# Two gate/up units split into gate and up steps, with two transposes between them

## The chip, the cores and the metric

The kernel runs on one core of one Trainium2 chip. The metric is the device time of one execution in microseconds (us). The kernel before was run three times: the median is 214.61 us, the lowest 214.41 us and the highest 215.21 us. One profiled execution took 214.28 us; the span that its profile shows, from the first to the last instruction, is 212.4 us. All times "at" which something happens are counted from the start of that span.

## The reference, cut to what matters

For 2048 tokens of width 512 the program normalises the rows, and adds three terms: the input itself, a linear attention (32 heads of 16, with exponential features), and a bilinear gated feed-forward of width 1792.

```python
x = A_x                                    # 1 x 2048 x 512, bf16
xn = _layernorm(x, axis=-1)                # (x - mean) / sqrt(var + eps), no weights
return x + _A_ref(xn, A_wqkv, A_w_phi, A_wo) + _B_ref(xn, B_w_gate, B_w_up, B_w_down)

def _B_ref(x, w_gate, w_up, w_down):       # w_gate, w_up: 512 x 1792; w_down: 1792 x 512
    g = jnp.einsum("bsd,df->bsf", x, w_gate)
    u = jnp.einsum("bsd,df->bsf", x, w_up)
    h = g * u
    return jnp.einsum("bsf,fd->bsd", h, w_down)

def _A_ref(x, wqkv, w_phi, wo):            # q, k, v = heads of x @ wqkv
    # features: softmax of +q w_phi and of -q w_phi (the same for k)  -> phi_q, phi_k
    # kv = phi_k^T v, z = sum of phi_k;  o = (phi_q kv) / (phi_q z)
    return o @ wo
```

The change lies in the first steps of the feed-forward: the products g and u of the first 256 tokens with two of the 14 column blocks of w_gate and w_up.

## The kernel before

The kernel is written as a list of named steps. Each step has an engine, a function, and the memory it reads and writes; the dependencies follow from these. A list scheduler then chooses the order of the steps on every engine, and `sc.chain("a b c")` forces a before b before c. The order is static: an engine takes its steps in that order and waits on semaphores in between. PSUM has 8 banks; a dependency is kept for a whole bank, whichever columns of it are touched.

PE is TensorE, DVE VectorE, ACT ScalarE, POOL GpSimd; SP issues most DMAs. A token tile t is 128 tokens, an FF tile ft is 128 of the 1792 columns. The normalised rows must be turned (transposed) before they can be multiplied. For token tiles 0 to 3 TensorE turns them, in two halves, each into a PSUM bank that ScalarE or VectorE then copies to SBUF (`xe`); for tiles 4 to 15 a DMA turns them (`xT`).

```python
def LN(ts, turn=True, ...):
    for t in ts:
        dve(bn_stats(...), name=f"st{t}")                       # 128x512
        dve(bn_aggr(...), name=f"ag{t}")
    act_op(lnv, var, func=Ln, bias=eps, name=f"ln{a}")          # rstd = exp(-0.5 ln(var + eps))
    act_op(rstd, lnv, func=Exp, scale=-0.5, name=f"rs{a}")
    for t in ts:
        if turn:                                                # token tiles 4 to 15
            pool(nb = -mean * rstd, name=f"nb{t}")
            act_op(xn = x * rstd + nb, name=f"nm{t}")
            sc.dma(SP, xnT, xn, turn=True, name=f"xT{t}")
            continue
        dve(xn = (x - mean) * rstd, name=f"nm{t}")              # token tiles 0 to 3

def T(t, split=False, banks=None):                              # turn by TensorE
    for hh, eng in ((0, ACT), (1, ACT if t == 0 else DVE)):
        b = nb() if banks is None else banks[hh]
        mm([... 2 matmuls of 128 columns against the identity ...], name=f"T{t}.{hh}")
        # ACT: name xe{t}a or xe{t}b;   DVE: name xe{t}d

def U2(ft, s_lo):                                               # 256 tokens, one FF tile
    b = nb()
    mm(group(bank(b, 0, 256),   [4 matmuls with w_gate])        # 8 matmuls of 256 columns, ONE bank
     + group(bank(b, 256, 256), [4 matmuls with w_up]), name=f"gu{ft}.{s_lo}")
    g = gring()[:, 0:256]
    act_op(g, bank(b, 0, 256), name=f"ge{ft}.{s_lo}")           # copy of the gate
    dve(h = bank(b, 256, 256) * g, name=f"h{ft}.{s_lo}")
# U1(ft, t): the same for one token tile (gu{ft}t{t}, ge{ft}t{t}, h{ft}t{t}; 8 matmuls of 128 columns)
# U(ft, sg): 512 tokens, gate and up in two banks (g{ft}.{sg}, u{ft}.{sg}, ge..., h...)
# ... (cut)

# the loads, in the order in which the DMA queue of SP takes them (u0 goes by ACT)
sc.chain("x0 x1 wg0 x2 wg2 wu2 wg4 wu4 wphi wT1 wv x4 wg8 wu8 x8 x12")
#   x2: token tiles 2, 3;  wg2, wu2: FF tiles 2, 3 of gate and up;  x4, x8, x12: four token tiles each

# the start
LN([0]); T(0, split=True); LN([1]); T(1, split=True)            # arguments cut
U1(0, 0); U1(1, 0); U1(0, 1); U1(1, 1)
LN([2], turn=False); LN([3], turn=False)
T(2, split=True, banks=(2, 3))
T(3, split=True, banks=(4, 5))
U2(2, 0); U2(3, 0)
rp[0] += 4
U1(0, 2); U1(1, 2); U1(0, 3); U1(1, 3); U2(2, 256); U2(3, 256)
# ... (cut: three chains, see the change)
# then: FF tiles 4 to 13 for 512 tokens (U), the folded key weights (F1), keys k0.. (K), values v0.. (V),
#       and blocks of the feed-forward by Strassen-Winograd, which need
#   XSUMS on VectorE (Xs0.0 to Xs3.1: sums of turned token tiles 4 to 11, so after xT11)
#   WSUMS on GpSimd  (gw.., uw..: sums of weight blocks)
#   b1..b7 on TensorE (b7g.0 ...), a4.., a5.. (additions) on VectorE, s.. copies on ScalarE
# K(t): k{t} on TensorE (4 matmuls of 512), ke{t} twice on ACT, kr{t} on DVE, kc{t} on ACT, kq{t}, kp{t} on POOL
# V(t): v{t} on TensorE, vs{t} on DVE, vz{t} on ACT;  KV(t): kv{t} on TensorE (needs kp{t}, vs{t})
```

Of the kernel before, what the change touches and what calls it, by code (L numbers as in the profile page):

```python
# [9 lines left out]
ALU = mybir.AluOpType  # L10
# [3 lines left out]
PE, ACT, DVE, POOL, SP = "PE", "ACT", "DVE", "POOL", "SP"  # L14
# [7 lines left out]
NQ = D // 128  # L22
# [352 lines left out]
def _build(nc, es, A_x, A_wqkv, A_w_phi, A_wo, B_w_gate, B_w_up, B_w_down, out):  # L375
# [65 lines left out]
    def bank(b, lo=0, n=512):  # L441
        return psum[:, b * 512 + lo: b * 512 + lo + n]

    sc = _Sched(nc)
# [49 lines left out]
    def mm(items, name=""):  # L494
        def fn(e):
            ins = None
            for (o, l, r, s, p) in items:
                ins = e.matmul(o, lhsT=l, rhs=r, start=s, stop=p, skip_group_check=True)  # L498
            return ins
        reads, writes, c = [], [], 0.0  # L500
        for o, l, r, s, p in items:
            track(o, s)
            reads += [l, r]
            writes.append(o)
            c += mm_cost(o.free_size())
        st = sc.step(PE, fn, reads=reads, writes=writes, cost=c, name=name)
        st.ns = tuple(o.free_size() for o, _, _, _, _ in items)
        return st

    def group(o, pairs):  # L510
        n = len(pairs)
        return [(o, l, r, i == 0, i == n - 1) for i, (l, r) in enumerate(pairs)]
# [12 lines left out]
    def xnT(q, s_lo, n):  # L525
        return xnT_v[:, q, s_lo:s_lo + n]

    wg_v = sbv("wg", 0, NQ * FF).rearrange("p (q f) -> p q f", q=NQ)
# [25 lines left out]
    def load_sq(eng, v, src, nbytes, name, after=None):  # L554
# [5 lines left out]
                      name="c")  # L560
# [76 lines left out]
    rp = [0]  # L637
# [15 lines left out]
    def T(t, split=False, banks=None):  # L653
        o = xnT_v[:, :, t * 128:(t + 1) * 128]
        if split:
            for hh, eng in ((0, ACT), (1, ACT if t == 0 else DVE)):
                b = nb() if banks is None else banks[hh]
                mm([(bank(b, q * 128, 128), xn_tile(t)[:, (2 * hh + q) * 128:(2 * hh + q + 1) * 128], ident, True, True)
                    for q in range(2)], name=f"T{t}.{hh}")
                oh = o[:, 2 * hh:2 * hh + 2, :]  # L660
                src = bank(b, 0, 256).rearrange("p (q s) -> p q s", q=2)
                if eng == ACT:
                    act_op(oh, src, name=f"xe{t}{'ab'[hh]}")
                else:
                    dve(lambda e, oh=oh, src=src: e.tensor_copy(out=oh, in_=src), [src], [oh], name=f"xe{t}d")
            return
        b = nb()
        mm([(bank(b, q * 128, 128), xn_tile(t)[:, q * 128:(q + 1) * 128], ident, True, True) for q in range(NQ)],
           name=f"T{t}")
        src = bank(b).rearrange("p (q s) -> p q s", q=NQ)  # L670
        if t % 2 == 0:
            act_op(o, src, name=f"xe{t}")
        else:
            dve(lambda e: e.tensor_copy(out=o, in_=src), [src], [o], name=f"xe{t}")
# [102 lines left out]
    def hs(s_lo):  # L777
        return s_lo % 1536
    gctr = [0]

    def gring():
        s = gctr[0] % 4
        gctr[0] += 1
        return sbv("gring", s * 512, 512)
# [132 lines left out]
    def U2(ft, s_lo):  # L917
        b = nb()
        mm(group(bank(b, 0, 256), [(wg_v[:, q, ft * 128:(ft + 1) * 128], xnT(q, s_lo, 256)) for q in range(NQ)])
           + group(bank(b, 256, 256), [(wu_v[:, q, ft * 128:(ft + 1) * 128], xnT(q, s_lo, 256)) for q in range(NQ)]),  # L920
           name=f"gu{ft}.{s_lo}")
        g = gring()[:, 0:256]
        act_op(g, bank(b, 0, 256), name=f"ge{ft}.{s_lo}")
        h = hT_v[:, ft, hs(s_lo):hs(s_lo) + 256]
        dve(lambda e: e.tensor_tensor(out=h, in0=bank(b, 256, 256), in1=g, op=ALU.mult), [bank(b, 256, 256), g], [h],  # L925
            name=f"h{ft}.{s_lo}")

    def U1(ft, t):
        b = nb()
        mm(group(bank(b, 0, 128), [(wg_v[:, q, ft * 128:(ft + 1) * 128], xnT(q, t * 128, 128)) for q in range(NQ)])  # L930
           + group(bank(b, 128, 128), [(wu_v[:, q, ft * 128:(ft + 1) * 128], xnT(q, t * 128, 128))
                                       for q in range(NQ)]), name=f"gu{ft}t{t}")
        g = gring()[:, 0:128]
        act_op(g, bank(b, 0, 128), name=f"ge{ft}t{t}")
        h = hT_v[:, ft, t * 128:(t + 1) * 128]
        dve(lambda e: e.tensor_tensor(out=h, in0=bank(b, 128, 128), in1=g, op=ALU.mult), [bank(b, 128, 128), g], [h],
            name=f"h{ft}t{t}")
# [166 lines left out]
    U1(1, 1)  # L1104
    LN([2], turn=False)
    LN([3], turn=False)
    T(2, split=True, banks=(2, 3))
    T(3, split=True, banks=(4, 5))
    U2(2, 0)
    U2(3, 0)  # L1110
    rp[0] += 4
    U1(0, 2)
    U1(1, 2)
    U1(0, 3)
    U1(1, 3)
    U2(2, 256)
    U2(3, 256)
    sc.chain("st0 ag0 st1 ag1 nm0.0 nm0.1 nm1 xe1d st2 ag2 h0t0 st3 ag3 nm2 h1t0 nm3 xe2d xe3d h0t1")
    sc.chain("T3.1 gu3.0")
    sc.chain("ln0 rs0 ln1 rs1 xe0a xe0b xe1a ge0t0 ln2 rs2 ge1t0 ln3 rs3 xe2a xe3a")  # L1120
    late = [len(sc.steps)]
    units = [(U, ft, 0) for ft in range(4, NF)]
    n0 = len(units)
# [166 lines left out]
```

The softmax here doesn't subtract the row's maximum and nothing guards it: scores larger than these inputs give would overflow.

## Time and profile before

| | |
|---|---|
| median of 3 runs | 214.61 us (214.41 to 215.21) |
| span of the profile | 212.4 us |
| granted TensorE clock | full speed in every slice |
| idle share: PE, DVE, ACT, POOL | 3%, 25%, 46%, 28% of the span |
| HBM read, written | 9.72 MB, 2.10 MB |
| costliest group | the matmuls: 201.2 us busy in 1597 records |
| next | GpSimd sums of 128x256 and larger (L766): 108.2 us busy in 96 records |

How to read it: an engine's busy share is an average over stages that have different limits, and a busy TensorE is not one at its peak, since matmuls are pipelined and their ends are modelled. A line of a timeline gives the start, the busy length, the engine, the line of the kernel and the shape; in brackets stand the idle time of the engine just before it and what ended that idle time. L498 is the line of every matmul, L451 of every ScalarE operation, L631 that of the normalising of token tiles 0 to 3 (`nm`), L796 that of `h` of U, L853 that of `a4` and `a5`, L925 that of `h` of U2, L716 that of `kp`. "SPq" is SP's queue that issues DMAs.

### The profile page before, as it was taken

How to read it: one execution, taken by the hardware profiler on the slowest of the kernel's cores; microseconds unless marked ns; L12 is line 12 of the kernel's file. 1: busy time of each engine (PE TensorE's matmuls, PEld its weight loads, DVE VectorE, ACT ScalarE, POOL GpSimd, SP SyncE). 2: the span in 40 equal slices, each digit the busy share in tenths (PEclk: the TensorE clock that was granted, in tenths of full speed). 3: DMA queues.
4: the chain of work that ended last, by engine and by line, in shares of the span. 5: the costliest groups of instructions: out<-in, count | busy, mean ns of one | idle time of the engine just before them, and what ended most of it. 6: DMA issues, size and time to landing. Idle time of an engine off the chain costs nothing.

```text
span 212.4 us, 4261 instructions
## 1 busy us (share of the span) xinstructions
PE 205.5 (97%) x1607; PEld 137.4 (65%) x1630; DVE 159.3 (75%) x313; ACT 113.8 (54%) x292; POOL 153.2 (72%) x191
## 2 busy tenths in 40 slices
PE   8799999999999999999999999999999999999995
PEld 3585444543454444444456788898888888888984
DVE  4655599899977698889987875686666876568653
ACT  4646998789796959697822533424433244332000
POOL 4060589359999999999999795875958779422640
PEclk9999999999999999999999999999999999999999
DMA  5999634793200000222620246143261434624421
GB/s 164 328 241 376 205 79 76 233 287 99 44 8 0 3 0 0 49 51 52 209 39 3 49 52 149 25 101 75 55 146 25 94 84 76 119 51 84 99 76 52
DMA packets 49718, 21.01 MB, mean 99 GB/s; under 512 B 37409, under 2 KB 49697, under 8 KB 49697
## 3 DMA queue, kind: packets, MB, share of 16 engines
q1 hardware_dynamic: 49024, 20.41, 39.9%
q10 hardware_dynamic: 672, 0.33, 0.6%
q8 instruction: 13, 0.21, 0.4%
q14 instruction: 9, 0.07, 0.1%
HBM read 9.72 MB, written 2.10 MB: 56 GB/s over the span
## 4 chain that ended last, share of the span: by engine, by line
PE 68%; POOL 23%; DMA 3%; issue 2%; SPq 1%; DVE 1%; ACT 0%; DVEq 0%; POOLq 0%
PE ps L498 68%; POOL arena L766 16%; POOL arena L716 6%; DMA arena<-in_B_w_up_dram 3%; POOL arena L714 1%; SPq L175 1%; DVE arena L925 0%; ACT arena L451 0%; POOL arena L621 0%; DVE arena L1015 0%; DVE arena L631 0%; DVEq L349 0%; DVE arena L1078 0%; POOLq L320 0%
## 5 line engine op out<-in xcount | busy, mean ns | idle before, releaser
L498 PE MATMUL ps<-arena 128*128 128x256 bf16 (+5 forms) x1597 | 201.2, 286 | 3.7 <-DVE arena L631 1.2
L498 PEld LDWEIGHTS ps<-arena 128*128 128x128 bf16 (+1 forms) x1620 | 136.0, 98 | 69.4 <-DVE arena L631 2.1
L766 POOL TENSOR_TENSOR arena<-arena 128x256 f16<-128x256 bf16 (+3 forms) x96 | 108.2, 1148 | 22.9 <-PE ps L498 16.9
L451 ACT ACTIVATE arena<-ps 128x512 bf16<-128x512 f32 (+3 forms) x167 | 83.7, 535 | 68.5 <-PE ps L498 66.5
L707 DVE TENSOR_REDUCE arena<-arena 128x64 f32<-128x1024 bf16 x32 | 38.7, 1211 | 9.4 <-ACT arena L451 9.4
L451 ACT ACTIVATE arena<-arena 128x32 f32<-128x32 f32 (+4 forms) x96 | 28.9, 317 | 12.8 <-DVE arena L707 10.2
L716 POOL TENSOR_TENSOR arena<-arena 128x512 bf16<-128x512 bf16 x32 | 34.2, 1072 | 0.7
L1015 DVE TENSOR_TENSOR arena<-ps,arena 128x256 f32<-128x256 f32 (+1 forms) x56 | 23.4, 420 | 12.6 <-PE ps L498 12.3
L925 DVE TENSOR_TENSOR arena<-ps,arena 128x256 f16<-128x256 f32 x32 | 13.4, 419 | 11.2 <-ACT arena L451 11.2
L847 DVE TENSOR_TENSOR arena<-ps,arena 128x512 f16<-128x512 f32 x24 | 16.1, 683 | 1.0 <-PE ps L498 0.8
L714 POOL TENSOR_TENSOR arena<-arena 128x32 f32<-128x32 f32 x32 | 8.7, 275 | 9.3 <-ACT arena L451 9.3
L612 DVE BATCH_NORM_STATS2 arena<-arena 128x6 f32<-128x512 bf16 x16 | 10.6, 674 | 3.4 <-DMA arena<-in_A_x_dram 3.4
L741 DVE TENSOR_TENSOR arena<-ps,arena 128x512 bf16<-128x512 f32 x16 | 10.8, 680 | 2.1 <-ACT arena L451 1.5
L796 DVE TENSOR_TENSOR arena<-ps,arena 128x512 f16<-128x512 f32 x14 | 9.5, 680 | 2.9 <-PE ps L498 1.8
L853 DVE TENSOR_TENSOR ps<-ps,arena 128x512 f32<-128x512 f32 x12 | 8.1, 694 | 4.4 <-PE ps L498 2.9
L973 DVE TENSOR_TENSOR arena<-ps,arena 128x512 bf16<-128x512 f32 x16 | 11.0, 688 | 0.4
L621 POOL TENSOR_SCALAR arena<-arena 128x1 f32<-128x1 f32 x12 | 3.5, 314 | 8.5 <-ACT arena L451 8.5
L853 DVE TENSOR_TENSOR arena<-ps,arena 128x512 bf16<-128x512 f32 x12 | 8.0, 678 | 0.0
L594 POOL TENSOR_TENSOR arena<-arena 128x128 bf16<-128x128 bf16 x4 | 1.6, 427 | 8.8 <-DMA arena<-in_A_w_phi_dram 8.8
L451 ACT ACTIVATE ps<-ps 128x512 f32<-128x512 f32 x12 | 7.2, 598 | 0.6 <-PE ps L498 0.6
L969 DVE RECIPROCAL arena<-arena 128x32 f32<-128x32 f32 x16 | 5.6, 351 | 0.4
L1092 PE MATMUL ps<-const-bfloat16-1.0 128*128 128x512 bf16 x10 | 4.4, 629 | 0.8 <-PEq L1275 0.8
(21 smaller groups left out, 27.9 us busy)
## 6 DMA issues: line engine op xcount, KB each, us to landing
arena<-in_A_x_dram SPq DMA_DIRECT2D x5, 512.0 KB, 6.9
arena<-in_B_w_down_dram SPq DMA_DIRECT2D x1, 1792.0 KB, 8.1
out_dram<-arena SPq DMA_DIRECT2D x14, 128.0 KB, 2.1
arena<-in_B_w_gate_dram SPq DMA_DIRECT2D x1, 768.0 KB, 8.5
arena<-in_B_w_up_dram SPq DMA_DIRECT2D x1, 768.0 KB, 10.0
arena<-arena SPq DMA_TRANSPOSE x44, 3.0
arena<-in_B_w_gate_dram SPq DMA_DIRECT2D x2, 256.0 KB, 4.7
arena<-in_B_w_gate_dram SPq DMA_DIRECT2D x1, 512.0 KB, 6.3
```

The lines of the kernel that those rows point to most:

```text
L451: return e.activation(out=out_ap, in_=in_ap, func=func, scale=scale, **kw)
L498: ins = e.matmul(o, lhsT=l, rhs=r, start=s, stop=p, skip_group_check=True)
L707: dve(lambda e, ei=ei, so=so: e.tensor_reduce(out=so, in_=ei.rearrange("p (h f) -> p h f", f=16), axis=AX.X, op=ALU.add), [ei], [so], cost ...
L714: pool(lambda e: e.tensor_tensor(out=ratio, in0=smv[:, :, 0], in1=rc, op=ALU.mult), [sm, rc], [ratio], 225.0, name=f"{name}q{t}")
L716: pool(lambda e: e.tensor_tensor(out=ev[:, :, 1, :], in0=ev[:, :, 1, :], in1=ratio[:, :, None].to_broadcast([128, H, 16]), op=ALU.mult), [ ...
L741: dve(lambda e: e.tensor_tensor(out=o1, in0=src, in1=rp_[:, :, :, None].to_broadcast([128, 8, 4, 16]), op=ALU.mult), [src, rs_v[:, t % 4, ...
L766: fn = lambda e: e.tensor_tensor(out=out_, in0=a_, in1=b_, op=op)
L847: dve(lambda e: e.tensor_tensor(out=h, in0=src, in1=g, op=ALU.mult), [src, g], [h], name=f"h{ft}.{sg}", prio=PD)
L853: dve(lambda e: e.tensor_tensor(out=o, in0=src, in1=sn, op=ALU.add), [src, sn], [o], name=name, prio=PD)
L925: dve(lambda e: e.tensor_tensor(out=h, in0=bank(b, 256, 256), in1=g, op=ALU.mult), [bank(b, 256, 256), g], [h], name=f"h{ft}.{s_lo}")
L973: dve(lambda e: e.tensor_tensor(out=ov, in0=src, in1=wv4[:, :, :, None].to_broadcast([128, 8, 4, 16]), op=ALU.mult), [src, w], [o], cost=6 ...
L1015: dve(lambda e: e.tensor_tensor(out=out_, in0=in_ps, in1=in_sb, op=ALU.add), [in_ps, in_sb], [out_], cost=328.0, name=f"{name}.{p}")
```

## The change

The first 256-token units of FF tiles 2 and 3 (`U2(2, 0)` and `U2(3, 0)`, 8 matmuls in one bank each) become four steps of 4 matmuls, gate and up in banks of their own. The two gate steps no longer need the up weights (`wu2`), which arrive one DMA later than the gate weights; the turns of token tiles 2 and 3 are put between the up steps. The chains for the three engines are rewritten: on TensorE the order is fixed outright; on ScalarE `rs3` (the scale of token tile 3) goes ahead of `ge2.0`; on VectorE `nm3` goes ahead of `h2.0`. The second half of token tile 2 is copied out by ScalarE (`xe2b`) and no longer by VectorE (`xe2d`). The numbers of the banks that follow shift by three places in the ring. It is meant to give TensorE work in its two early waits.

```diff
     def T(t, split=False, banks=None):
-            for hh, eng in ((0, ACT), (1, ACT if t == 0 else DVE)):
+            for hh, eng in ((0, ACT), (1, ACT if t in (0, 2) else DVE)):
...
+    def GU2(fts, s_lo, bg, bu, order):
+        g = {ft: gring()[:, 0:256] for ft in fts}
+        for w, ft in order:
+            if w == "T":
+                T(ft, split=True, banks=bu["T"][ft])
+                continue
+            b = bank((bg if w == "g" else bu)[ft], 0, 256)
+            v = wg_v if w == "g" else wu_v
+            mm(group(b, [(v[:, q, ft * 128:(ft + 1) * 128], xnT(q, s_lo, 256)) for q in range(NQ)]),
+               name=f"{w}{ft}.{s_lo}h")
+            if w == "g":
+                act_op(g[ft], b, name=f"ge{ft}.{s_lo}")
+            else:
+                h = hT_v[:, ft, hs(s_lo):hs(s_lo) + 256]
+                dve(lambda e, h=h, b=b, gg=g[ft]: e.tensor_tensor(out=h, in0=b, in1=gg, op=ALU.mult), [b, g[ft]], [h],
+                    name=f"h{ft}.{s_lo}")
...
     LN([2], turn=False)
     LN([3], turn=False)
-    T(2, split=True, banks=(2, 3))
-    T(3, split=True, banks=(4, 5))
-    U2(2, 0)
-    U2(3, 0)
-    rp[0] += 4
+    GU2((2, 3), 0, {2: 0, 3: 1}, {2: 4, 3: 5, "T": {2: (2, 7), 3: (3, 6)}},
+        [("g", 2), ("g", 3), ("u", 2), ("T", 2), ("u", 3), ("T", 3)])
+    rp[0] += 7
...
-    sc.chain("st0 ag0 st1 ag1 nm0.0 nm0.1 nm1 xe1d st2 ag2 h0t0 st3 ag3 nm2 h1t0 nm3 xe2d xe3d h0t1")
-    sc.chain("T3.1 gu3.0")
-    sc.chain("ln0 rs0 ln1 rs1 xe0a xe0b xe1a ge0t0 ln2 rs2 ge1t0 ln3 rs3 xe2a xe3a")
+    sc.chain("g2.0h g3.0h u2.0h T2.0 T2.1 u3.0h T3.0 T3.1 gu1t2")
+    sc.chain("st0 ag0 st1 ag1 nm0.0 nm0.1 nm1 xe1d st2 ag2 h0t0 st3 h1t1 ag3 nm2 h1t0 nm3 h0t1 h2.0 xe3d h3.0")
+    sc.chain("ln0 rs0 ln1 rs1 xe0a xe0b xe1a ge0t0 ln2 rs2 ge1t0 ln3 rs3 ge2.0 xe2a xe2b xe3a ge3.0")
```

The orders that the scheduler makes of it at the start are these (names of steps; no times are in them):

```
TensorE before:  gu0t0 gu1t0 gu0t1 gu1t1 | gu2.0 | T2.0 T2.1 | T3.0 T3.1 | gu3.0 | gu1t2 gu0t2 gu0t3 gu1t3 gu2.256 gu3.256
TensorE after:   gu0t0 gu1t0 gu0t1 gu1t1 | g2.0h g3.0h | u2.0h | T2.0 T2.1 | u3.0h | T3.0 T3.1 | gu0t2 gu1t2 gu0t3 gu1t3 gu2.256 gu3.256
ScalarE before:  ... ge1t0 ln3 ge2.0 rs3 xe2a xe3a ge3.0 ...
ScalarE after:   ... ge1t0 ln3 rs3 ge2.0 xe2a xe2b xe3a ge3.0 ...
VectorE before:  ... nm2 h1t0 h2.0 nm3 xe2d xe3d h0t1 h3.0 ...
VectorE after:   ... nm2 h1t0 nm3 h0t1 h2.0 xe3d h3.0 ...
```

The same scheduler places everything that follows, so later orders move too. On TensorE the sequence from kv4 to v14 is the same in both, k1 moves ahead of u8.0, and a few steps near kv14, kv15 and n0 to n2 change places. On ScalarE and GpSimd the keys' steps, the weight sums and the normalising of tiles 4 to 15 are interleaved differently: on ScalarE the two `ke0` now stand together ahead of `nm4`, `nm12` stands behind `kc3l` (the first half of `kc3`) and `nm13` behind `s7g.0`; on GpSimd `nb8` stands behind `gw2.0` as before, but with `gw3.1` moved ahead of it, and `S1.0` (a sum for the last product) stands ahead of `kq4` and no longer behind it.

## The prediction

> **What bounds the kernel now.** I read the page first, then the timeline of the first 16 us, then the waits and the timeline of each engine up to 96 us. The first part of the page says which engine is full:
>
> ```profile
> PE 205.5 (97%) x1607; PEld 137.4 (65%) x1630; DVE 159.3 (75%) x313; ACT 113.8 (54%) x292; POOL 153.2 (72%) x191
> ```
>
> TensorE is idle for 6.9 us in all. So the change can win only where TensorE is idle, and what it wins counts only if TensorE doesn't idle later instead. The chain of work that ended last agrees: 68% of it is TensorE, 23% GpSimd, which stands in it from 42 to 95 us. The timeline of the start shows the two waits that the change aims at:
>
> ```profile
> 8.64 1.27 PE L498 MATMUL ps<-arena 128*128 128x256 bf16 x12 [0.52 <-DMA arena<-in_B_w_up_dram]
> ...
> 8.81 0.38 DVE L631 TENSOR_SCALAR arena<-arena 128x512 bf16<-128x512 bf16 x1
> 8.93 0.29 ACT L451 ACTIVATE arena<-arena 128x1 f32<-128x1 f32 x1 [0.23 <-DVE arena L614]
> 9.11 0.28 DVE L936 TENSOR_TENSOR arena<-ps,arena 128x128 f16<-128x128 f32 x1
> 9.73 0.38 ACT L451 ACTIVATE arena<-ps 128x256 bf16<-128x256 f32 x1 [0.51 <-PE ps L498]
> 10.01 0.19 ACT L451 ACTIVATE arena<-arena 128x1 f32<-128x1 f32 x1
> ...
> 10.14 0.42 DVE L925 TENSOR_TENSOR arena<-ps,arena 128x256 f16<-128x256 f32 x1 [0.76 <-ACT arena L451]
> 10.48 0.40 DVE L631 TENSOR_SCALAR arena<-arena 128x512 bf16<-128x512 bf16 x1
> ...
> 10.94 21.24 PE L498 MATMUL ps<-arena 128*128 128x128 bf16 x146 [1.03 <-DVE arena L631]
> ```
>
> In brackets stands the idle time and what ended it. TensorE waits 0.52 us for the up weights (gu2.0), and 1.03 us for nm3, the row at 10.48. That row is late because ScalarE did ge2.0 (9.73) before rs3 (10.01), and VectorE did h2.0 (10.14) before nm3. After 10.94 TensorE hardly idles; the later waits, from the timelines of SP, VectorE and TensorE, are these:
>
> ```profile
> 31.21 6.25 SPq L174 DMA_TRANSPOSE arena<-arena  x4
> ...
> 38.77 1.43 DVE L766 TENSOR_TENSOR arena<-arena 128x512 f16<-128x512 bf16 x4 [0.55 <-DMA arena<-arena]
> ...
> 42.88 5.55 PE L498 MATMUL ps<-arena 128*128 128x512 bf16 x31 [0.27 <-DVE arena L796]
> 48.67 1.68 PE L498 MATMUL ps<-arena 128*128 128x512 f16 x7 [0.23 <-DVE arena L853]
> ...
> 95.36 1.51 PE L498 MATMUL ps<-arena 128*128 128x68 bf16 x12 [0.17 <-POOL arena L716]
> ```
>
> The reader should see a second chain: turns xT8 to xT11 by DMA, then the sums Xs0.0 to Xs1.1 on VectorE at 38.77, then h13.0, for which k5 on TensorE waits, then a4g.0, for which b7u.0 waits. By stretches:
>
> ```profile
> 26.00:38.00 12.00, 11.95 (x56) 5.46 (x56) 12.00 (x24) 11.01 (x30) 11.21 (x21) 1.00 0.41 78
> 38.00:39.00 1.00, 1.00 (x7) 0.47 (x5) 0.46 (x2) 1.00 (x3) 0.00 (x0) 1.00 0.28 33
> 39.00:52.00 13.00, 12.50 (x78) 5.82 (x78) 13.00 (x23) 11.05 (x31) 8.07 (x12) 1.00 0.89 242
> 52.00:62.00 10.00, 9.89 (x69) 4.94 (x70) 7.98 (x13) 8.78 (x21) 10.00 (x18) 1.00 0.14 28
> ```
>
> The columns after the length are PE, PEld, DVE, ACT, POOL. VectorE has no idle time from 26 to 38 us and from 39 to 52 us, 12.00 of 12 and 13.00 of 13. There it is as much a bound as TensorE is, and the only gap between is the wait for xT11. That decides my prediction.
>
> **What the Trainium skill says.** "PSUM — Partial Sum Buffer", section "Engine vs sequencer instructions": the queues of ScalarE, VectorE and GpSimd are strictly first in, first out, and matmuls start and complete in program order. The trace agrees: nm3 sat behind h2.0 and TensorE idled 1.03 us. "Perfetto Trace Analysis", section "Matmuls": independent groups should rotate through PSUM banks, so that one is read out while the next is computed. Here ge2.0 starts at 9.73, after all eight matmuls of gu2.0 (the last ends at 9.69), although its four were done sooner; banks of their own end that. "TensorE: Matmul & The Clock Gate", section "Wait — 56ns, not 53.3ns?": a warm matmul takes N / 2.4 GHz plus 2.5 ns, so 56 ns for 128 columns and 109 ns for 256, an estimate from that page. The trace agrees: eight of 256 and four of 128 come to 1.10 us, and the row at 8.64 shows 1.27 us with the tail of the last one (0.22 us).
>
> **The change, part by part.** Matmuls, copies and multiplications stay as many as before; one 128x256 copy moves from VectorE (0.42 us) to ScalarE (0.38 us), and that work isn't on the path. So only waits move. I walk the new orders with the durations above.
>
> Start. The last matmul of gu1t1 is issued at 7.91, and wg2 landed at 7.8 (issued at 2.75, 5.0 us). So g2.0h and g3.0h run from 7.97 to 8.84, 8 x 0.109. wu2 landed at 8.60: u2.0h to 9.28. T2 needs nm2, which ends at 9.19: T2 to 9.50. u3.0h to 9.94 (its bank is freed by h1t0 at 9.39). rs3 now follows ln3 at once and ends at 9.46; nm3 runs after h1t0 from 9.52 to 9.91; T3.0 starts at 9.96; T3.1 waits for h0t1 (to 10.11) and is issued by 10.27. On ScalarE ge2.0, xe2a and xe2b then follow at 9.38, 9.67 and 9.96 + 0.38 = 10.34, so gu0t2 starts at 10.39. In the kernel before the same work (gu1t2) starts at 12.05, which is 10.94 + 4 x 0.056 + 8 x 0.109. Gain so far 1.65 us: the two waits are 0.52 + 1.03 us by the brackets, and 0.16 us more each from issue to issue, since the brackets leave out the tail of the matmul before (1.87 us); about 0.2 us are lost to new waits for nm3, h0t1 and xe2b.
>
> From 14 to 37 us. The weights wg4 to wu8 land before they are needed (wu8 at 23.4, u8.0 at 24.3), k0 still finds fe13 just ready, and I find no new wait over 0.25 us. TensorE stays 1.4 to 1.65 us ahead.
>
> The chain of token tiles 8 to 11 doesn't come with it. x4 lands at 19.19 and x8 at 24.81 (issued at 14.38, 10.4 us), whatever TensorE does. On ScalarE ln4 starts at 21.3, not at 21.87, since it waits for x4 by st4, st5 and ag5. On VectorE st8 moves from 26.56 to 26.0. On GpSimd nb8 stands behind gw3.0, gw1.0, gw3.1 and gw2.0 (0.64 us each), which wait for nm7 (26.8): nb8 ends at 30.0. So nm8 starts at 30.1 and not at 30.36, and the four turns of SP, which take 6.25 us in a row and are bound by themselves after the first, start 0.25 us sooner. xT11 lands at 38.5 and not at 38.75.
>
> From 38.5 to 49 us. VectorE has the same work in the same order up to kr4: h13.0 ends 3.83 us after the start of Xs0.0 (42.60 - 38.77), so at 42.3. TensorE reaches k5 at 41.0 and waits 1.3 us. There the gain falls from about 1.4 to 0.25 us. Then st15 (0.6 us) comes ahead of a4g.0 and vs4 behind it, which cancel, and nm13 delays sdg.0 on ScalarE; b7u.0 starts at 48.5 and not at 48.67. I keep 0.15 us.
>
> At 95.36. TensorE waits for kp12; its previous matmul was issued 0.36 us before and takes 0.03, so kv12 could start at 95.03. GpSimd is full from 49 us on, so its order decides. Adding the durations of the trace before in each order from the first of kq4 and S1.0 to the end of kp12 gives 48.1 us before and 47.2 us after. S1.0 may start at 47.15 (after xT13, which is late because nm13 is), 0.27 us later than kq4 did. So kp12 ends some 0.6 us sooner, and the wait of 0.3 us goes. Slacks of kv13 to kv15 and n0 to n3 are 0.3 to 2.5 us before, and I find none that turns into a wait.
>
> Sum: 0.15 + 0.3 = 0.45 us, from 214.61 to 214.15 us.
>
> **The rivals.** First: the gain of the start goes through whole. For it speaks that TensorE is full after 11 us and the DMA weights are early. Against it stands VectorE's 13.00 of 13 us, which begins with a landing that doesn't move. It would be so if the turns took less: xT8's issue took 2.3 of the 6.25 us, the other three 1.3 each, and without that the landing comes 1.1 us sooner. It would make 213.0 to 213.4 us. Second: the start is won and lost twice, because ScalarE now waits for kr3 (behind kc3l) ahead of nm12 and ke4, so that b1g.0 and b2g.0 wait in their turn, and S1.0 holds kq4 back until xT13. It would leave nothing or cost up to 0.5 us: 214.6 to 215.1 us. Third: T3.1's and xe2b's waits are longer than walked, so that the start gains 1 us and not 1.65. It changes nothing at the end, because 1.3 us are waited away at k5.
>
> **Range and chances.** I expect 214.15 us. The first rival reaches to 213.2, the second to 214.9, and I give the middle most of the weight. 2% are 4.3 us, nearly three times what TensorE could gain even if both waits went whole; and no step adds work. So within 2% is all but sure: 0.98.
>
> **What would show it.** In the profile after: no idle time of TensorE from 8 to 9.5 us, and at most 0.3 us to 10.5; the first 128-column matmuls after T3 at about 10.4. Idle time of VectorE before Xs0.0 over 1 us, ended by a DMA, with Xs0.0 at 38.5. TensorE idle over 1 us before k5, at about 42.4, ended by L796. No wait for L716 near 95. I am wrong if Xs0.0 starts before 37.8 (first rival), or if TensorE has idle time over 0.3 us at more places than k5 between 42 and 62 us (second rival).

## The result, and the profile after

| kernel | median | lowest to highest | executions |
|---|---|---|---|
| before | 214.65 us | 214.16 to 215.21 | 6 |
| after | 213.28 us | 212.32 to 213.53 | 6 |

The medians lie 1.37 us apart, where 0.45 us had been predicted. The ratio is 0.9929, with a 95% interval of 0.9903 to 0.9954; ratios in this document are not quotients of the medians (0.9936 here), so the two differ a little. The profile of the kernel after is of the slowest of its six executions (213.53 us), that of the kernel before of one of 214.28 us. In the chain of work that ended last, which the page gives by engine, GpSimd had 23% of the span and has 4% now; TensorE has 78% instead of 68%. This is that line of the kernel after:

```profile
PE 78%; ACT 7%; DMA 5%; POOL 4%; DVE 3%; issue 1%; SPq 0%; DVEq 0%
```

The start, from the timeline of TensorE (first row) and that of all engines in the kernel after (start, duration, engine, line, operands; idle time before it in brackets):

```profile
6.80 6.46 PE L498 MATMUL ps<-arena 128*128 128x128 bf16 x90
...
9.35 0.53 ACT L451 ACTIVATE arena<-arena 128x1 f32<-128x1 f32 x2 [0.19 <-DVE arena L614]
...
9.78 1.30 ACT L451 ACTIVATE arena<-ps 128x256 bf16<-128x256 f32 x4
9.91 0.41 DVE L631 TENSOR_SCALAR arena<-arena 128x512 bf16<-128x512 bf16 x1
```

The reader should see that TensorE's row runs from 6.80 to 13.26 us without a bracket. Both waits of the kernel before (0.52 us at 8.64, 1.03 us at 10.94) are gone. ln3 and rs3 stand together at 9.35, ahead of ge2.0 at 9.78, and nm3 starts at 9.91 instead of 10.48.

The later rows that answer to those shown of the kernel before, from the timelines of SP, VectorE and TensorE:

```profile
30.54 5.13 SPq L174 DMA_TRANSPOSE arena<-arena  x4
...
36.98 1.84 DVE L766 TENSOR_TENSOR arena<-arena 128x512 f16<-128x512 bf16 x4 [0.22 <-DMA arena<-arena]
...
47.24 9.93 PE L498 MATMUL ps<-arena 128*128 128x512 f16 x52 [0.31 <-DVE arena L853]
57.49 2.82 PE L498 MATMUL ps<-arena 128*128 128x512 bf16 x25 [0.33 <-ACT ps L451]
89.75 10.61 PE L498 MATMUL ps<-arena 128*128 128x512 bf16 x62
```

The four turns xT8 to xT11 are issued in 5.13 us and not in 6.25 us, and start 0.67 us sooner. So the sums on VectorE (36.98) start 1.79 us sooner than in the kernel before (38.77). There is no wait worth a row at k5 (0.10 us from issue to issue), a longer one at b7u.0 (47.24), a new one at b2u.1 (57.49, for ScalarE), and none near 94 us, where the kernel before waited for kp12. Putting the starts of single steps of TensorE side by side gives the account:

| step | before | after | difference | what lies between |
|---|---|---|---|---|
| gu0t0 | 6.18 | 6.64 | +0.46 | wg0 landed at 6.55 and not 6.09 |
| first of gu0t2, gu1t2 | 12.05 | 10.76 | -1.29 | both early waits gone |
| kv1, the step ahead of k5 | 42.20 | 40.92 | -1.28 | nothing lost in 30 us |
| k5 | 42.66 | 41.27 | -1.39 | its wait for h13.0 shrank from 0.2 to 0.1 us |
| b7u.0 | 48.67 | 47.24 | -1.43 | wait for a4g.0 in both |
| b2u.1 | 58.43 | 57.49 | -0.94 | new wait, 0.49 us from issue to issue |
| kv12 | 95.36 | 94.11 | -1.25 | wait for kp12 (0.33 us from issue to issue) gone |
| last group (W22.7) | 209.58 | 208.32 | -1.26 | |

In the kernel before the record of k5's first matmul is missing; its weight load stands at 42.65, and the row at 42.88 is the second matmul.

By stretches (columns after the length: PE, PEld, DVE, ACT, POOL busy) the kernel after is:

```profile
26.00:38.00 12.00, 12.00 (x57) 5.44 (x56) 11.78 (x24) 11.32 (x29) 10.65 (x19) 1.00 0.45 89
...
39.00:52.00 13.00, 12.69 (x73) 5.63 (x72) 12.52 (x20) 11.61 (x32) 7.54 (x12) 1.00 0.73 203
```

VectorE is still all but full there, as the prediction had it. What was wrong is when its work arrives.

### The profile page after: what moved, and what is told of

Its sections match the earlier page's. It is cut to its first block, busy times and chain, and to the rows that moved or that the text cites. A ratio compares the mean times of both kernels' runs of the same rounds, so it can differ in the third digit from the quotient of the medians.

```text
span 211.2 us, 4288 instructions
## 1 busy us (share of the span) xinstructions
PE 206.6 (98%) x1630; PEld 137.1 (65%) x1630; DVE 159.9 (76%) x312; ACT 114.3 (54%) x293; POOL 153.1 (73%) x191
## 4 chain that ended last, share of the span: by engine, by line
PE 78%; ACT 7%; DMA 5%; POOL 4%; DVE 3%; issue 1%; SPq 0%; DVEq 0%
PE ps L498 78%; ACT arena L451 6%; DMA arena<-arena 3%; DMA arena<-in_B_w_gate_dram 2%; POOL arena L766 2%; POOL arena L716 1%; DVE arena L612 1%; DVE arena L766 1%; DVE arena L707 1%; SPq L175 0%; DVE arena L796 0%; POOL arena L714 0%; ACT ps L451 0%; DVE arena L614 0%; DVE arena L1032 0%
## 5 line engine op out<-in xcount | busy, mean ns | idle before, releaser
L498 PE MATMUL ps<-arena 128*128 128x512 bf16 (+5 forms) x1620 | 202.4, 287 | 1.3 <-DMA arena<-in_B_w_gate_dram 0.4
L498 PEld LDWEIGHTS ps<-arena 128*128 128x128 bf16 (+1 forms) x1620 | 135.7, 98 | 68.4 <-ACT arena L451 2.2
L451 ACT ACTIVATE arena<-ps 128x512 bf16<-128x512 f32 (+3 forms) x168 | 83.3, 533 | 66.0 <-PE ps L498 62.8
L451 ACT ACTIVATE arena<-arena 128x64 f32<-128x64 f32 (+4 forms) x96 | 28.5, 314 | 14.2 <-DVE arena L707 10.9
L925 DVE TENSOR_TENSOR arena<-ps,arena 128x256 f16<-128x256 f32 x30 | 12.6, 418 | 9.5 <-ACT arena L451 9.5
L451 ACT ACTIVATE ps<-ps 128x512 f32<-128x512 f32 x12 | 7.2, 600 | 0.0
```

The source lines that it names most:

```text
L451: return e.activation(out=out_ap, in_=in_ap, func=func, scale=scale, **kw)
```

## Why xT8 is quicker: the theories

xT8 is of the same size in both kernels. From its issue to its landing it takes 4.31 us before (31.21 to 35.52) and 2.41 us after (30.54 to 32.95). The DMA view of the kernel before, for the 4 us from the issue of xT8 in 40 slices of 0.1 us (busy share in tenths, then GB/s, then the kinds of packets):

```profile
DMA  0000810000006999999601000000001000003999
GB/s 0 0 0 0 164 82 0 0 0 0 0 8 138 212 228 215 205 156 123 15 8 5 5 18 10 10 15 5 0 5 8 3 0 0 0 0 82 215 210 236
...
q8 instruction: 1, 0.02, 2.2%
q14 instruction: 2, 0.02, 2.2%
```

And the same for the kernel after, from 30.5 us on:

```profile
DMA  0000030000004999995200000399999520000029
GB/s 0 0 0 0 0 82 0 0 0 0 0 0 90 210 228 225 212 207 115 24 0 0 0 0 0 72 200 225 223 212 215 133 32 0 0 0 0 0 51 197
...
q14 instruction: 1, 0.01, 0.8%
```

After, each turn is one burst of 0.7 us, and the next follows 1.3 us later. Before, the burst of xT8 ends in a trickle of 3 to 18 GB/s, from 33.1 to 34.4 us, the next burst only comes at 34.8, and xT8 is complete inside it, at 35.52. In the same window lies a packet of q8 (16 KB in slice 5, the 164 GB/s). The page counts 13 packets of q8. "Runtime: NRT & Kernel Launch", section "Instruction fetch mechanics", of the Trainium skill says that a sequencer fetches its instructions by a DMA queue of its own, in blocks of 16 KiB or 256 instructions. TensorE has 1,630 matmuls and as many weight loads, 3,260 or 12.7 blocks, so q8 should be TensorE's. The traces agree: the second packet of q8 comes when 208 to 214 weight loads have started, the warm-up's included, which with as many matmuls are 416 to 428 instructions, in all fourteen profiled executions, and in the kernel before the packets after it follow 254 instructions apart in the mean. q14 carries packets of 8 KB; that they are the other engines' is taken from their size and not shown. TensorE's block was fetched at 31.66 us before, 0.45 us after the issue of xT8, and at 30.21 us after, 0.33 us ahead of it.

Theory A: a fetch that falls into a turn holds it up. The fetch goes with TensorE's place in its program, so the change moves it out of xT8. Theory B: landings vary by chance. Theory C: the new order of everything after 14 us brings xT8 forward. Later, rival D: the whole gain is the moved fetch and the change has no part in it.

## The experiments on the fetch

**The kernel before once more, unchanged.** It shows how far executions of one program differ.

> The kernel before, unchanged, profiled a second time. Theory A (the turn xT8 took 2.3 us in the first profile because an instruction fetch of TensorE fell into it, which the order of the program fixes): xT8 takes about 2.3 us again, the four turns xT8 to xT11 6.2 us in a row, Xs0.0 on VectorE starts at 38.5 to 39. Theory B (the landing of the loads x4 and x8 varies from execution to execution, and the first profile caught a late one): xT8 takes 1.2 to 1.3 us or x4 lands a microsecond elsewhere, and Xs0.0 starts at 37 to 38. Time: ratio 1.000 in both.

Measured: 214.23 us (213.25 to 215.19, 22 executions), ratio 1.0002 [0.9990, 1.0014]. The profiled execution was its quickest (213.25 us). In it the fetch fell at 32.09, xT8 took 4.39 us to land, but xT9 to xT11 lost less, and xT11 landed at 38.12 and not 38.75. VectorE, which has work up to that moment, didn't wait at all, nor did TensorE at k5 or b7u.0, and W22.7 started at 208.55, 1.03 us sooner. So executions of one program lie up to 1.9 us apart, and in the quickest the turns landed sooner, with the fetch inside xT8 all the same: what counts for the time is when xT11 lands. Half of the 22 lie between 214.0 and 214.5 us: chance is real, and does not explain a median that moves.

**The fetch moved in the kernel before.** Six more, shorter warm-up matmuls bring TensorE's block limit forward; everything else is the same.

```diff
-    WARM(10)     # matmuls of 512 columns
+    WARM(16)     # matmuls of 320 columns
```

> The kernel before with its warm-up of 10 matmuls of 512 columns cut into 16 of 320: the same columns in the same time, but 6 matmuls and 6 weight loads more ahead of everything, so that TensorE's instruction fetch that came at 31.7 us comes about 1.3 us sooner, at 30.4, ahead of xT8 at 31.2. All orders are those of the kernel before. Theory A: xT8 takes 1.2 us, Xs0.0 starts about 1.1 us sooner (37.6), the waits at k5 and b7u.0 shrink, and the time falls by 0.5 to 0.9 us (ratio 0.9958 to 0.9977). Theory B and theory C (the new order after 14 us is what brings xT8 forward): ratio 1.000.

Measured: 213.30 us (212.93 to 213.48, 6 executions), ratio 0.9954 [0.9942, 0.9965]. The fetch came at 30.88; xT8 landed after 3.52 us, xT11 at 37.91. VectorE had no gap before Xs0.0 (38.07), and the waits at k5 and b7u.0 were gone. The timeline of SP:

```profile
31.13 5.49 SPq L174 DMA_TRANSPOSE arena<-arena  x4
```

The start is as it was (g4.0 at 15.51, 15.58 before). The ratio is a little better than theory A said, without a line of the change: B falls, and C isn't needed for this part. But the steps came short of what A said: the fetch lay 0.25 us ahead of xT8 and not 0.8, the issue of xT8 took 1.53 us and not 1.2, and Xs0.0 started at 38.07 and not 37.6.

**The fetch moved back in the kernel after.** The warm-up is three matmuls shorter and starts later.

```diff
-    WARM(10)
+    WARM(7)      # and the first waits for a constant
```

> The changed kernel with a warm-up of 7 matmuls and no longer 10, the first held back until GpSimd has made a mask (at about 2.2 us), so that it ends when it ended before; 3 matmuls and 3 weight loads fewer, so that TensorE's fetch at 30.2 comes about 0.65 us later, at 30.9, inside xT8 (30.5 to 31.7). All orders are those of the changed kernel. Theory A: xT8 takes 2.3 us, xT11 lands 1.1 us later, TensorE waits about 1 us at k5, and the time is 0.6 to 1.1 us over that of the changed kernel (ratio to the kernel before 0.9965 to 0.999). Theory B and C: the time of the changed kernel (ratio 0.993).

Measured: 212.89 us (212.51 to 213.64, 6 executions), ratio 0.9939 [0.9924, 0.9955]. The median misses what A expected and is what B and C expected. But the profiled execution was the slowest of the six (213.64 us), and in it the fetch fell into xT8, at 32.17. Its timelines:

```profile
30.95 6.20 SPq L174 DMA_TRANSPOSE arena<-arena  x4
...
38.45 1.43 DVE L766 TENSOR_TENSOR arena<-arena 128x512 f16<-128x512 bf16 x4 [1.29 <-DMA arena<-arena]
...
42.57 5.42 PE L498 MATMUL ps<-arena 128*128 128x512 bf16 x31 [0.82 <-DVE arena L796]
48.29 11.92 PE L498 MATMUL ps<-arena 128*128 128x512 f16 x73 [0.30 <-DVE arena L853]
```

This is the picture that was predicted: the turns in 6.2 us, VectorE idle for over 1 us before Xs0.0, which starts at 38.45 (predicted 38.5), TensorE waiting 0.82 us at k5 (over 1 us predicted), b7u.0 at 48.29 (predicted 48.5). So the prediction described an execution that this order can have when the fetch falls into xT8. The other five were 0.36 to 1.13 us quicker; where their fetch fell was not profiled.

**The fetch moved further, in both kernels.** Twenty warm-up matmuls of 256 columns, in one set of runs on one chip, so that the change can be compared with itself.

```diff
-    WARM(10)     # matmuls of 512 columns
+    WARM(20)     # matmuls of 256 columns, in before and in after
```

> The kernel before with its warm-up as 20 matmuls of 256 columns (ten instructions more), so that TensorE's instruction block is fetched near 30.4 us, clear ahead of the issue of xT8 at 31.15. Theory A (only a fetch that falls into the turn holds it): xT8 lands 2.4 us after its issue as in the kernel after (4.3 us in the kernel before), xT11 by 37.5 us; but VectorE has work up to 38.07 us anyway, so the time is that of the edit with 16 matmuls, 0.994 to 0.9965 of the kernel before, with W22.7 at 208.4 to 208.6. Rival B (landings vary by chance, the fetch has no part): xT8 lands 3.5 to 4.4 us after its issue and the time is 0.998 to 1.001.

> The kernel after with the same warm-up of 20 matmuls; the fetch falls near 28.9 us, into xT7, which nothing waits for yet. With the kernel before under the same edit, on the same chip, this gives what the change gains when neither has the fetch in xT8. Theory A: 0.3 to 0.7 us less than the kernel before with 20 matmuls, 0.991 to 0.994 of the kernel before. Rival D (all of the gain was the fetch): no difference within 0.15 us. Rival E (the change gains as much with the fetch out of the way, and the fetch's gain comes on top): over 1.0 us less.

Measured: the kernel before 214.47 us; before with 20 matmuls 213.33 us (213.24 to 213.47, 6 executions), 0.9939 [0.9915, 0.9962]; after with 20 matmuls 212.52 us (211.84 to 212.86, 5 executions), 0.9891 [0.9859, 0.9922]. Between the two edited kernels lie 0.81 us, and no execution of one reaches the other's range. So D falls. The value lies between what A and E expected, over A's 0.7 and under E's 1.0 us by the medians; between the two profiled executions (W22.7 at 208.59 and 207.40) it is 1.19 us. In round numbers, of 1.95 us 1.14 come with the shifted fetch and 0.81 with the change. In the kernel after without this edit the two can't be cut so cleanly, since the change itself moves the fetch. One expectation missed: with 20 matmuls in the kernel before, xT8 took 3.38 us and not 2.4. The fetch now fell into xT7 (4.17 us), which landed 1.37 us after xT8 was issued, and two packets of q14 fell into xT8; which of the two held it was not separated. The timeline of TensorE in the kernel after with 20 matmuls:

```profile
6.80 6.40 PE L498 MATMUL ps<-arena 128*128 128x128 bf16 x86
...
46.83 13.45 PE L498 MATMUL ps<-arena 128*128 128x512 f16 x82 [0.31 <-DVE arena L853]
```

Here wg0 landed at 6.08, gu0t0 started at 6.23, and the gain at the start is 1.68 us (g4.0 at 13.91, 15.59 without the change). The wait at b2u.1 didn't occur. The wait at b7u.0 remains: with smaller ones before it, it takes the lead over the kernel before with 20 matmuls from 1.68 us at kv1 to 0.85 us at b7u.0; at b2u.1 the lead is 1.06 us.

**The kernel after with 16 matmuls.**

> The kernel after, with only the warm-up of TensorE written as 16 matmuls of 320 columns instead of 10 of 512 (same columns, six instructions more), so that TensorE's instruction block is fetched some 0.9 us earlier. The kernel before with the same edit was at 0.9954 [0.9942, 0.9965] of the kernel before. Theory A (the change gains by itself, and the fetch only takes from it what it hits): 0.989 to 0.993 of the kernel before, 0.6 to 1.2 us under the kernel before with the same edit, and no different from the kernel after, whose fetch already lies before xT8. Rival D (the whole gain of the change was that its six extra or earlier instructions moved the fetch): 0.995 to 0.996, no faster than the kernel before with the same edit.

Measured: 212.94 us (212.71 to 213.49, 7 executions), 0.9936 [0.9913, 0.9959]. That lies between what A (up to 0.993) and D (from 0.995) expected, and the 0.9954 of the kernel before with the same edit comes from another chip; so this run by itself leaves D open, and the pair above was run. In the profiled execution wg0 landed late (7.02 us, gu0t0 at 7.11). The fetch fell into xT7, which took 4.28 us and which nothing waited for; xT8 took 2.40.

All profiled executions together, by what was fetched between 0.3 us ahead of xT8's issue and its landing:

| fetched beside xT8 | executions | issue to landing of xT8, us | issue of xT8 to landing of xT11, us |
|---|---|---|---|
| one q14, no q8 | 4 (after; after with 16 and 20; after tuned) | 2.41, 2.40, 2.64, 2.40 | 6.41, 6.40, 6.67, 6.40 |
| q8 within 0.3 us ahead, or two q14 | 3 (before with 16 and 20; last version below) | 3.52, 3.38, 3.20 | 6.77, 6.77, 6.78 |
| q8 up to 1.3 us after the issue | 7 (before, twice; after with 7; the other four below) | 4.30, 4.39, 4.11, 3.31, 4.10, 4.08, 4.04 | 7.53, 6.94, 7.48, 7.30, 7.32, 7.53, 7.26 |

The last column is what Xs0.0 waits for. It is not the order of the engines that parts the rows: with the order of the kernel after it is 6.40 to 6.67 us in the four without the fetch and 7.48 us in the one with it (7 matmuls). The limit of 0.3 us was drawn with the results in view: the kernel after has its fetch 0.33 us ahead of xT8 and the turn isn't held, the last version has it 0.27 us ahead and it is. Four of the seven had two packets of q14 besides; the three with one took 4.11, 3.31 and 4.04 us.

And xT7 took 2.46 to 2.48 us in eleven of the fourteen; in the three where TensorE's block was fetched beside it, it took 4.28, 4.17 and 3.86.

## The experiments on the parts of the change

In these kernels and in those of the next part, the orders of all engines are fixed by a list, so that only the named steps move; line numbers shift for it (TensorE's L498 is L585 to L587, ScalarE's L451 is L538 to L540).

**The new start with the old order from 14 us on.** On TensorE, ScalarE and VectorE the order of the kernel before from g4.0, ge4.0 and h4.0 on, on GpSimd and SP throughout.

```diff
- ... the scheduler's order after the change
+ sc.pin(PIN)   # start as after; from g4.0 / ge4.0 / h4.0 on as before
```

> The changed kernel with its new start, but from g4.0, ge4.0 and h4.0 on (and on GpSimd and SP throughout) in the order of the kernel before. Theory A: TensorE's fetch comes at about 30.2 with TensorE 1.3 to 1.7 us ahead, xT8 at 30.6 to 31.2, so they don't meet; xT11 lands by 37.6 and the ratio is 0.993 to 0.996. Theory C (the new order of ScalarE and GpSimd after 14 us brings xT8 and xT11 forward): TensorE waits about 1 us at k5 and the ratio is 0.997 to 1.000. Theory B: anything between.

Measured: 212.71 us (212.39 to 213.06, 5 executions), 0.9926 [0.9913, 0.9938]. That is the ratio of the kernel after. Theory C falls: the new order downstream isn't needed. Theory A is close in the ratio and missed a step: the fetch at 30.16 did meet xT8, which was issued at 29.77 and took 3.31 us. The timelines of SP and VectorE:

```profile
29.77 6.02 SPq L174 DMA_TRANSPOSE arena<-arena  x4
...
37.10 1.43 DVE L854 TENSOR_TENSOR arena<-arena 128x512 f16<-128x512 bf16 x4 [0.37 <-DMA arena<-arena]
```

The four turns took 6.02 us, and Xs0.0 still came at 37.10, because nm8 started at 28.93 us (before 30.36, after 29.72), though GpSimd's order was that of the kernel before.

**Only the two orders, no split.**

```diff
-    ... ln3 ge2.0 rs3 xe2a ...      (ScalarE)      ... h2.0 nm3 ...   (VectorE)
+    ... ln3 rs3 ge2.0 xe2a ...      (ScalarE)      ... nm3 h2.0 ...   (VectorE)
```

> The kernel before, all orders pinned as they were, but rs3 ahead of ge2.0 on ScalarE and nm3 ahead of h2.0 on VectorE. Nothing is split, no bank changes. Theory A (waits are what counts, and one of the two can be taken without the split): nm3 ends near 9.9 us, T3.0 starts at about 9.96 instead of 10.94, the wait of 0.52 us for the up weights stays, g4.0 starts at about 14.5 instead of 15.58, gain about 1.0 us at the start; at the end 0.4 to 1.0 us less than the kernel before, ratio 0.9953 to 0.998. Rival (the reorder only hands the wait on, because h2.0 then holds gu3.0's bank or T2's copies): T3.0 near 10 us but g4.0 not under 15.2 us, ratio over 0.998.

Measured: 213.09 us (212.35 to 213.37, 6 executions), 0.9930 [0.9905, 0.9956]. T3.0 started at 9.80 and g4.0 at 14.52, as theory A said; at the end it gained more than A said. The timeline of TensorE:

```profile
8.58 3.63 PE L585 MATMUL ps<-arena 128*128 128x256 bf16 x43 [0.57 <-DMA arena<-in_B_w_up_dram]
...
47.60 14.57 PE L585 MATMUL ps<-arena 128*128 128x512 f16 x99 [0.24 <-DVE arena L940]
```

The wait for wu2 stays, the one for nm3 is gone, and the ratio can't be told from that of the kernel after. Here too the fetch fell into xT8 (4.10 us). Two swaps of neighbours do, as the kernel stands, what the split does.

**Only the split.** ge2.0 ahead of rs3 and h2.0 ahead of nm3 as in the kernel before, and its order from g4.0 on; split, banks and TensorE's order as after.

```diff
-    ... ln3 rs3 ge2.0 ...           (ScalarE)      ... nm3 h0t1 h2.0 ...   (VectorE)
+    ... ln3 ge2.0 rs3 ...           (ScalarE)      ... h2.0 nm3 h0t1 ...   (VectorE)
```

> The kernel after with its split, banks and TensorE order, but ge2.0 ahead of rs3 on ScalarE and h2.0 ahead of nm3 on VectorE as in the kernel before, and the order of before from g4.0 on. Theory A (splitting the units fills both waits even without the other order, because ge2.0 is ready 0.9 us sooner when the gate step has a bank of its own): T3.0 at about 10.3 us, g4.0 at 14.25 to 14.5 us, gain at the start 1.1 to 1.3 us; ratio 0.992 to 0.995. Rival (the order of nm3 is what counts, the split alone only moves the wait to T3): T3.0 at 10.7 us or later, g4.0 at 14.9 or later, ratio over 0.996.

Measured: 213.30 us (213.06 to 213.59, 8 executions), 0.9949 [0.9931, 0.9968]. wu2 landed late (9.23 us, 8.60 before), so that u2.0h waited. T3.0 came at 10.88, as late as the rival said, g4.0 at 14.73, between the two, and the time is A's.

The three show one more thing. With the order of the kernel before downstream, g4.0 came 1.49, 1.06 and 0.85 us sooner than in the kernel before, and nm8 came 1.43, 1.08 and 0.86 us sooner: one for one. In the order of the kernel after it is 1.28 and 0.65 us (with 20 matmuls 1.68 and 1.04 against the edited kernel before). The chain of token tiles 8 to 11 does come along; the new order (gw3.1, 0.67 us, stands ahead of nb8 there) only holds back some 0.6 us of it. And it follows TensorE, not the load: with the fetch shifted and nothing else, in the kernel before, x4 landed at 17.84 us (16 matmuls) and 18.19 us (20 matmuls) and no longer at 19.19, and ln4, the first step of token tiles 4 and 5 on ScalarE, came at 21.79 and 21.87 us (21.87 before), and xT8 was issued at 31.13 and 31.22 us.

## The experiments on what is given back

**The kernel after with three pairs of steps moved.**

```diff
-    ag14 st15 kr5 a4g.0 vs4 a5g.0 ag15 h0.1 kr6           (VectorE)
+    ag14 kr5 a4g.0 vs4 a5g.0 h0.1 kr6 st15 ag15
-    s2g.1 nm14 nm15 ke7 ke7 sdu.1 ge1.2 s7u.1 kc7l s2u.1 sdg.2          (ScalarE)
+    s2g.1 ke7 ke7 sdu.1 ge1.2 s7u.1 kc7l s2u.1 nm14 nm15 sdg.2
```

> The kernel after, its orders pinned, with st15 and ag15 moved behind kr6 on VectorE (so that a4g.0 is done 0.6 us sooner) and nm14 and nm15 moved behind s2u.1 on ScalarE. Theory A (the waits of 0.48 us at b7u.0 and 0.49 us at b2u.1 are what the change gives back): both waits go, W22.7 starts 0.5 to 0.9 us sooner than in the kernel after, ratio 0.989 to 0.991. Rival (VectorE and GpSimd are full there and hand the wait on: a5g.0, or tiles 14 and 15 come late): waits of the same size at b5u.0, at the steps of tiles 14 and 15, or at kv12, and a ratio of 0.992 to 0.995, as the kernel after.

Measured: 213.72 us (213.43 to 214.22, 22 executions), 0.9972 [0.9963, 0.9982]: slower than the kernel after. The rival came true in kind, at other places than it named and at a higher price (it had said 0.992 to 0.995). The timeline of TensorE:

```profile
51.43 8.04 PE L587 MATMUL ps<-arena 128*128 128x512 bf16 x56 [0.35 <-ACT ps L540]
60.48 1.70 PE L587 MATMUL ps<-arena 128*128 128x512 bf16 x12 [1.01 <-ACT ps L540]
```

The wait at b7u.0 fell from 0.48 to 0.07 us and that at b2u.1 went. In their place TensorE waits for sdg.1 (ln14 ahead of it now waits for ag15) and for sdg.2 (nm14 and nm15 now stand ahead of it). Both edits won their wait and paid for it on the same engine a few steps on, 1.9 us in all with a small wait at F0 behind them.

**The old order downstream, tuned, with and without the shifted fetch.**

```diff
-    ke5 kc4l kc4 ge0.1 s2g.0 sdu.0   (ScalarE)   kr5 vs4 a4g.0   (VectorE)   kq4 S1.0   (GpSimd)
+    ke5 ge0.1 s2g.0 sdu.0 kc4l kc4   (ScalarE)   kr5 a4g.0 vs4   (VectorE)   S1.0 kq4   (GpSimd)
```

> The start of the kernel after with the order of before from g4.0 on, and three moves: on ScalarE ge0.1, s2g.0 and sdu.0 ahead of kc4l and kc4, which wait for kr4 of VectorE; on VectorE a4g.0 ahead of vs4; on GpSimd S1.0 ahead of kq4. Theory A (ScalarE stood 1.10 us before kc4l while s2g.0 was ready, and that made the waits of 0.34 us at b5g.0 and 0.40 us at b7u.0): the wait at b5g.0 goes, that at b7u.0 falls under 0.15 us, S1.0 starts at 44.8 us instead of 45.6, so GpSimd's kp12 comes about 0.6 us sooner too, W22.7 at 207.3 to 207.7, ratio 0.989 to 0.992. Rival (the wait is handed on as in the other tuned version): waits of over 0.3 us between 48 and 62 us or over 0.6 us at kv12, no faster than 0.9926.

> The same with the warm-up as 16 matmuls of 320 columns. Theory A (the fetch at 30.16 us still held xT8, which landed 3.3 us after its issue): the fetch comes near 29.3 us, xT8 lands near 32.2 us, VectorE doesn't wait before Xs0.0 (0.37 us), and the time is another 0.1 to 0.4 us down: ratio 0.987 to 0.991. Rival (GpSimd's chain up to kp12 sets the end by now): the same time as without the warm-up, the difference standing as a longer wait at kv12.

Measured: 212.92 us (212.24 to 213.23, 6 executions), 0.9912 [0.9886, 0.9937]; with 16 warm-up matmuls 212.64 us (212.26 to 212.87, 4 executions), 0.9902 [0.9873, 0.9932]. In the first the waits at b5g.0 and b7u.0 are gone and kv12 waits 0.12 us instead of 0.28 us; a new one of 0.49 us stands at b3g.0, for a5g.0 on VectorE. W22.7 started at 207.40 and 207.75. Both ratios, and W22.7 of the first, lie where A put them; the rival's sign, a wait of over 0.3 us near 48 us, came too. Apart from the version with three pairs moved, which is slower, the intervals of all versions overlap that of the kernel after, so none is shown to beat it; the lowest is the kernel after with 20 warm-up matmuls, 212.52 us. In the second the fetch did come earlier (29.69 us, 29.92 in the first), but not near 29.3: it lay 0.27 us ahead of xT8, which took 3.20 us and landed at 33.17, not near 32.2 as expected; VectorE had no gap before Xs0.0 all the same.

## Why the prediction was wrong in size, by its own steps

0.45 us were predicted, 1.37 us came: the direction, the start and the end at kv12 were right, one input of the sum was not, and with it the wait of 1.3 us that was to take the gain away.

**Start: right.** 10.39 us was predicted for the first 128-column work after T3, a gain of 1.65. The kernel after had 10.76, because wg0 landed 0.46 us late and gu0t0 with it; with wg0 on time (20 matmuls) it was 10.36, and g4.0 gained 1.68 us.

**14 to 37 us: right.** TensorE kept its lead, -1.28 at g4.0 and still -1.28 at kv1.

**"The chain of token tiles 8 to 11 doesn't come with it": this step failed.** It made the landing of xT11 38.5 us; it was 36.95. Two terms were mis-sized. The issue of xT8 came 0.67 us sooner and not 0.25 (nm8 0.65): I took x4's landing (19.19) as fixed, and so as the bound on ln4 (21.3 us). It was 18.20 us; over the fourteen profiled executions it lies between 17.5 and 19.2, so I had read the latest one as a constant. At 18.20 it bounds nothing: ln4 came at 20.61 us, 6.31 us after g4.0, and it comes 6.31 us after g4.0 in the three variants of the kernel after with another warm-up too. The second term is larger: "the four turns of SP, which take 6.25 us in a row" took 5.13 us, and TensorE's fetch no longer fell into xT8. 0.67 + 1.12 is the 1.79 us by which Xs0.0 came sooner; 0.25 had been predicted. In the runs with the old order downstream the first term does most of it: the fetch falls into xT8, and xT8 is issued 1.44 us (whole new start) and 1.07 us (two swaps) sooner than in the kernel before.

**38.5 to 49 us: the mechanism right, its input wrong.** h13.0 ended 4.2 us after Xs0.0 (3.83 predicted), but from 36.98 on, so k5 waited 0.10 and not 1.3 us. 0.15 us were to remain at b7u.0; 1.43 remained. In the execution where xT8 was hit (the kernel after with 7 matmuls) the step holds: h13.0 ended 3.83 us after Xs0.0 started.

**kv12: right, with more room than predicted.** The wait of 0.33 us (0.3 predicted) went. kp12 ended 1.26 us sooner (94.05 and 95.31), where some 0.6 had been predicted: from the first of kq4 and S1.0 to its end GpSimd took 47.35 us and no longer 48.43, and began 0.18 us sooner, where 0.27 us later had been predicted.

**The rivals.** The first, that the gain goes through whole "if xT8's issue took 1.3 and not 2.3 us", came true in its condition (1.19 us), in its sign (Xs0.0 before 37.8; it was 36.98) and in its time (213.0 to 213.4 predicted, 213.28 measured). I had seen the odd 2.3 us, and took it for a property of the program instead of asking what else ran on the DMA engines in that window. Of the second only the sign came, idle time over 0.3 us at other places than k5: 0.31 us at b7u.0 and 0.33 at b2u.1, which waits for ScalarE behind nm14, nm15 and ke7. At the places that it named, b1g.0 and b2g.0, TensorE didn't wait over 0.04 us. The third did not occur.

What stays open: how much of its 1.37 us the kernel after owes to the fetch as it stands. The two are not additive, and were only cut with the fetch shifted in both kernels; that the ratio of the kernel after is also reached with the fetch inside xT8 (0.9926 and 0.9930, in the executions profiled) suggests that it isn't needed. Whether the trickle is one DMA engine of 16 that serves the fetch first (3 to 18 GB/s against up to 228 in the burst) is argued, not shown; the profile keeps the engines together. And whether the split adds to the two swaps when the fetch is out of the way wasn't tried.

## What to carry to other kernels

Before a duration from one execution is put on the path as fixed, compare it with its siblings in the same trace: three turns took 1.3 us each and one took 2.3, and the odd one was a good part of the error. Where an engine is full for 25 us, ask first when its input arrives, and let the input move with its producers unless a view shows that it can't. And where several engines are nearly full, try two neighbours in another order before new structure (here it came out the same), and look at the steps that then stand behind: two moves here won their waits and lost more a few steps on.

## What the runs showed of the hardware that was not expected

**Instruction fetches delay DMA turns.** The section of the skill named above says that the fetch is hidden by the pace at which instructions are issued. For TensorE that fits: no wait of it in these traces is put down to a fetch. But a turn between two places in SBUF that takes 2.4 to 2.5 us to land took 3.2 to 4.4 us with TensorE's fetch or two smaller ones beside it, and with the engine behind it full this began what moved a whole program by 1 us; the next paragraph has the rest.

**VectorE and GpSimd shut each other out.** "SBUF — State Buffer", section "Who interferes with whom", of the skill says that a VectorE instruction with two inputs in SBUF and a GpSimd instruction that reads SBUF exclude each other for the whole instruction, and that the one that starts first wins. The rows agree. The kernel before, timelines of VectorE and GpSimd:

```profile
43.72 1.38 DVE L766 TENSOR_TENSOR arena<-arena 128x512 f16<-128x512 bf16 x2
...
43.42 1.06 POOL L716 TENSOR_TENSOR arena<-arena 128x512 bf16<-128x512 bf16 x1
```

The kernel before with 20 warm-up matmuls:

```profile
43.08 0.75 DVE L766 TENSOR_TENSOR arena<-arena 128x512 f16<-128x512 bf16 x2
...
43.09 0.86 POOL L714 TENSOR_TENSOR arena<-arena 128x32 f32<-128x32 f32 x1
```

The sums Xs3.0 and Xs3.1 take 1.38 us where GpSimd's kp3 had started first, and 0.75 us where they had; there GpSimd's small kq3 took 0.86 us instead of its 0.27. (In the first of the last two versions kp3's row starts 0.02 us ahead of the sums, and yet it is kp3 that is held, 1.68 us.) It is the other half of what the shifted fetch gained in the kernel before: with 20 matmuls Xs0.0 starts 0.62 us sooner, the pair takes 0.63 us less, a4g.0 starts 1.05 us sooner, and the wait at b7u.0 is gone; with 16 matmuls and in the quick execution of the unchanged kernel it is the same, 0.76 and 0.75 us for the pair. In the kernel after the pair takes 1.33 us, with and without the 20 matmuls. That is 0.58 us of VectorE's time just ahead of a4g.0, for which b7u.0 waits 0.48 us, and would account for most of the fall from 1.68 to 0.85 us of lead in the runs with 20 matmuls. An order for the kernel after that avoids this meeting alone was not tried.
